# A layer of attention and two of a network in one kernel: first-layer weights summed on VectorE, products ahead of the first attention, another order of the steps

## The chip, the cores and the metric

The kernel runs on one core of one Trainium2 chip. The metric is the device time of one execution in microseconds (us). A core has TensorE (PE in the profile; its weight loads are PEld), VectorE (DVE), ScalarE (ACT), GpSimd (POOL) and SyncE (SP), each with its own queue of instructions, which it works through in order. DMA transfers are issued from SP, ACT and POOL.

## The reference

A gated linear attention is followed by two layers with a PReLU between them. All is float32. B = 4, H = 8, S = 768, D = 48; the network has 3072 tokens of width H*D = 384, and 2048 hidden units.

```python
f = 1.0 / (1.0 + np.exp(-f_logit))
for t in range(S):
    state = f[:, :, t, :, None] * state + np.einsum('bhd,bhe->bhde', k[:, :, t], v[:, :, t])
    y[:, :, t] = np.einsum('bhd,bhde->bhe', q[:, :, t], state)
x = y.transpose(0, 2, 1, 3).reshape(B * S, H * D)
h = x @ w_in
g = np.maximum(h, 0.0) + alpha * np.minimum(h, 0.0)
return g @ w_out
```

## The kernel before

The tokens are cut into chunks of C = 128, and two batch entries are worked on together. That gives 12 steps, `(bp, c)`: two pairs of batch entries in each of six chunks. A step has four stages, each a generator that yields between its parts:

- `prepare` (L260) loads q, k, f and v. It makes the products of the gates within groups of four tokens (`qd`, L289), two running products (`ps`, `ss`, L319 and L321), and scaled queries and keys (`us`, `k4`, `q3`, `kh`, `ks`; L323 to L408). In chunks after the first it transposes the keys on VectorE (`kt`, L424) and spreads them with 16 small DMAs from SP into `ksn` (L429). In first chunks `ksn` comes from TensorE transposes (`pk`, L473).
- `carry` (L434) has the products `off` (L446, and L456 in first chunks), copies them to the attention matrix `A` on ACT, and carries the state: products `pd` (L486), then `moved`, which updates `vs` (L496, L500; L502 on ACT in first chunks).
- `attend` (L508) has, for each of the two batch entries, the small products `raw` (L522) and `qu` (L537), which VectorE copies under masks into `ad` (L528, L543; L559 in first chunks). These PSUM tiles ("pair") have two buffers in rotation with `off`, `pk`, `pd` and `py`. ACT then copies `ad` to `A` (L565), `py` (L576) multiplies with `vs`, and `y` (L585) is brought to the network's layout `xT`: by products `xt` (L594) in step 0, by DMAs from SP and ACT (L604) later.
- `network` (L610) has eight parts f, each with products `ph` (L619) into a PSUM bank, one ReLU on ACT (L624) and two gates on VectorE (L626). Step 0 then uses plain products `po` (L639) with `w_out_sb`; later steps use seven products of half width (`pa` to `pe`, L658) with sums made on VectorE (L700, L671 to L685). The banks ("net") have four buffers in rotation.

The network of a step runs in the next step, beside the attention of that step and the first half of `prepare` of the one after. The order is written out by hand: `manual_schedule` keeps TensorE, VectorE and ACT to the order of the program, and a string of letters for each of the first four steps, `first`, and one for the rest, `usual`, says which generator goes on next. P is the rest of this step's `prepare`, O `carry`, S `attend`, n the network of the step before, Q the next step's `prepare`. A number repeats. `a` and `w` are the two halves of loading `w_in`, `b` and `v` those of `w_out`, and W makes the sums of `w_out` (L719) that the half-width products need.

The weights are loaded in eight pieces each. They come from DRAM as int16 words (SP, L196, four buffers `raw`), ACT makes two parts of the upper half of the bits (L201, L203), and VectorE makes `lead` (L209), the scaled rest (L222) and its `power` (L215). At last `lead` is added to the rest, in `both`: by VectorE (L227) for pieces under `at_once`, otherwise by an accumulating DMA from POOL (L229). `AT_ONCE` (L27) counts for `w_in` alone. Part f of the first network needs piece f of `w_in`; a quarter of its `po` needs two pieces of `w_out`.

## Time and profile before

| | us |
|---|---|
| median of 3 runs (lowest to highest) | 637.01 (636.58 to 639.63) |
| the profiled execution's own time | 638.33 |
| its span, first to last instruction | 636.5 |
| TensorE products busy | 589.7 (93%) |
| TensorE weight loads busy | 524.9 (82%) |
| VectorE busy | 505.8 (79%) |
| ACT busy | 249.6 (39%) |
| POOL busy | 67.6 (11%) |

Times in the profile count from the first instruction. A row of a timeline has the start, the time to the end of the group, the engine, the line, the operation, out<-in with their shapes, and how many instructions follow each other. In brackets stands the engine's idle time before them and what ended it; "issue" is time in which it waited for nothing that the profile shows. A row of the waits has the waiting line, what it waited for, the total in us, how often, and the longest. A row of the chain of waits has start, us, and what the end of the program depended on then. A float32 product of the program is recorded as two products; a transpose is recorded as one.

### The profile page before, as it was taken

The numbers are of one execution on the slowest core, as the hardware profiler recorded it, in microseconds if no ns is written. First come the engines' busy times: TensorE is split into PE (matmuls) and PEld (weight loads), VectorE is DVE, ScalarE is ACT, GpSimd is POOL, SyncE is SP. The second block draws the span as 40 slices with busy tenths as digits, with TensorE's granted clock in tenths as the row PEclk, the third lists the DMA queues.
The fourth block names the chain that finished last, engine by engine and source line by source line (L and its number), as shares of the span: only waits on it lengthen the run. The fifth ranks groups of instructions, "written<-read, shape, count | busy, mean of one in ns | idle before, by whom it ended". The sixth has DMA issues, their size and how long they took to land.

```text
span 636.5 us, 18857 instructions
## 1 busy us (share of the span) xinstructions
PE 589.7 (93%) x8108; PEld 524.9 (82%) x8108; DVE 505.8 (79%) x1028; ACT 249.6 (39%) x466; POOL 67.6 (11%) x114
## 2 busy tenths in 40 slices
PE   0449699989999999999999999999999999999997
PEld 0447576779889889889889889889889889889997
DVE  5879959999799788888888888888888888762251
ACT  5667673432254153253253253253253253223120
POOL 9133212001001001001001001001001000000000
PEclk9999989999999999999999999999999999999999
DMA  7978978233232323223233233223233211201000
GB/s 260 280 199 235 287 198 199 46 77 78 43 83 84 43 77 83 51 69 83 38 81 85 38 82 84 38 82 84 33 85 79 46 47 26 37 18 26 26 1 25
DMA packets 73122, 56.30 MB, mean 88 GB/s; under 512 B 47408, under 2 KB 64944, under 8 KB 73040
## 3 DMA queue, kind: packets, MB, share of 16 engines
q0 software_dynamic: 10112, 27.53, 16.4%
q1 hardware_dynamic: 57536, 25.37, 15.7%
q10 hardware_dynamic: 5392, 2.21, 1.7%
q8 instruction: 64, 1.05, 0.7%
q14 instruction: 18, 0.15, 0.1%
HBM read 36.21 MB, written 4.72 MB: 64 GB/s over the span
## 4 chain that ended last, share of the span: by engine, by line
PE 75%; DVE 14%; SPq 3%; issue 3%; ACT 2%; DMA 1%; DVEq 0%; ACTq 0%
PE ph L619 33%; PE pc L658 8%; PE pa L658 8%; PE pe L658 4%; PE pd L658 4%; PE pb L658 4%; SPq L429 3%; PE py L576 3%; PE raw L522 3%; PE qu L537 2%; PE pd L486 2%; DVE gate L626 1%; DVE ad L528 1%; DVE us L332 1%; DVE ad L543 1%
## 5 line engine op out<-in xcount | busy, mean ns | idle before, releaser
L619 PE MATMUL ph<-xT,w_in_sb 128*128 128x256 f32 x1152 | 260.9, 385 | 5.1 <-issue 4.9
L619 PEld LDWEIGHTS ph<-xT,w_in_sb 128*128 128x128 f32 x1152 | 218.2, 192 | 38.4 <-issue 7.3
L624 ACT ACTIVATE neg<-ph 128x512 f32<-128x512 f32 x96 | 57.1, 597 | 203.1 <-PE ph L619 144.0
L626 DVE SCALAR_TENSOR_TENSOR gate<-neg,om,ph 128x256 f32<-128x256 f32 x192 | 82.1, 476 | 48.4 <-ACT neg L624 48.2
L658 PE MATMUL pa<-w_out_sb,gate 128*128 128x192 f32 x352 | 62.1, 329 | 0.3 <-DVE gate L626 0.3
L658 PE MATMUL pc<-t,S 128*128 128x192 f32 x352 | 61.8, 329 | 0.1
L658 PEld LDWEIGHTS pa<-w_out_sb,gate 128*128 128x128 f32 x352 | 57.8, 190 | 2.2 <-DVE gate L626 1.3
L658 PEld LDWEIGHTS pc<-t,S 128*128 128x128 f32 x352 | 57.3, 190 | 1.1 <-DVE Csum L671 0.4
L528 DVE COPY_PREDICATED ad<-mraw,raw 128x256 f32<-128x256 int32 (+1 forms) x96 | 42.3, 440 | 8.3 <-PE raw L522 5.9
L543 DVE COPY_PREDICATED ad<-mquad,qu 128x224 f32<-128x224 int32 (+6 forms) x140 | 41.9, 299 | 6.2
L419 ACT COPY A<-q 48x512 f32<-48x512 f32 x44 | 27.2, 617 | 31.6 <-DVE q L370 31.2
L565 ACT COPY A<-ad 32x256 f32<-32x256 f32 x96 | 38.5, 401 | 1.4
L332 DVE TENSOR_TENSOR us<-us,fs 128x768 f32<-128x768 f32 (+5 forms) x60 | 37.0, 617 | 0.0
L289 DVE TENSOR_TENSOR qd<-qd,f 128x768 f32<-128x768 f32 (+2 forms) x36 | 27.2, 756 | 6.7 <-ACT qd L284 6.7
L576 PEld LDWEIGHTS py<-A,vs 128*64 128x64 f32 x768 | 25.5, 145 | 7.2 <-ACT A L565 4.3
L576 PE MATMUL py<-A,vs 128*64 128x64 f32 x768 | 27.5, 232 | 3.9 <-ACT A L565 3.9
L522 PEld LDWEIGHTS raw<-qd,k 48*32 48x32 f32 x1536 | 18.7, 109 | 14.9 <-issue 13.9
L700 DVE TENSOR_TENSOR S<-gate 128x512 f32<-128x512 f32 x44 | 30.3, 688 | 0.8
L676 ACT COPY o<-pa 128x192 f32<-128x192 f32 x11 | 3.5, 317 | 69.7 <-PE pa L658 65.4
L522 PE MATMUL raw<-qd,k 48*32 48x80 f32 x1536 | 23.9, 243 | 7.3 <-issue 5.6
L658 PE MATMUL pe<-w_out_sb,S 128*128 128x192 f32 x176 | 30.5, 327 | 0.0
L658 PE MATMUL pd<-w_out_sb,S 128*128 128x192 f32 x176 | 30.4, 326 | 0.0
(109 smaller groups left out, 749.8 us busy)
## 6 DMA issues: line engine op xcount, KB each, us to landing
w_out_raw<-in_w_out SPq DMA_DIRECT2D x8, 767.8 KB, 6.0
w_in_raw<-in_w_in SPq DMA_DIRECT2D x8, 767.2 KB, 5.8
f<-in_fT POOLq DMA_DIRECT2D x11, 512.0 KB, 4.4
q<-in_qT POOLq DMA_DIRECT2D x11, 512.0 KB, 4.0
k<-in_kT POOLq DMA_DIRECT2D x11, 512.0 KB, 5.1
out<-o SPq DMA_DIRECT2D x24, 192.0 KB, 2.1
vs<-in_v POOLq DMA_DIRECT2D x22, 192.0 KB, 5.2
w_out_sb<-w_out_lead POOLq DMA_DIRECT2D x8, 384.0 KB, 5.4
```

What stands on the lines that cost most here:

```text
L289: nc.vector.tensor_tensor(qdv[d], qdv[d - 1][:, :, :, 1:5 - d], f[:, :, 1:5 - d].rearrange("p (g i) r -> p g i r", i=NB), ALU.mult)
L332: nc.vector.tensor_tensor(us[:, :, UO[m]:UO[m] + 4 * n].rearrange("p g (i r) -> p g i r", r=4), us[:, :, skip:skip + 4 * n].rearrange("p g ...
L522: nc.tensor.matmul(raw[DB * j:DB * (j + 1), par, hp * C:hp * C + QW], lhsT=k[r_, g * DB:(g + 1) * DB], rhs=qd[r_, g], start=True, stop=True)
L528: nc.vector.copy_predicated(adu[:, :, :, d:4], mraw[:, d, :, d:4].bitcast(I32).unsqueeze(1).broadcast_to((128, H, NB, n)), rv[:, :, QO[d]: ...
L543: nc.vector.copy_predicated(ad[:, u, :, :, 4 * m:DB], mquad[:, lo:lo + n].bitcast(I32).unsqueeze(1).unsqueeze(1).broadcast_to((128, 2, HP, ...
L565: nc.scalar.copy(A[s_, u, :, s_], ad[s_, u].rearrange("p r h t -> p (r h) t"))
L576: nc.tensor.matmul(py[64 * par:64 * par + 64, u, o:o + CH], lhsT=vs[bp][:, cc, u, hd * D:hd * D + 64], rhs=A[:, u, par * HP + hp, CH * cc: ...
L619: nc.tensor.matmul(ph[:, j * T:(j + 1) * T], lhsT=w_in_sb[:, kt, m * 128:(m + 1) * 128], rhs=xT[:, kt], start=(kt == 0 and j == 0), stop=( ...
L624: nc.scalar.activation(neg, phv, AF.Relu, scale=-1.0)
L626: nc.vector.scalar_tensor_tensor(gate[:, m % NH, m // NH], neg[:, j], om[:, m:m + 1], phv[:, j], ALU.mult, ALU.add)
L658: nc.tensor.matmul(to[:, 0:DH], lhsT=of(f), rhs=by(f), start=(f == 0 and not more), stop=(f == NH - 1), skip_group_check=True)
L700: nc.vector.tensor_tensor(to, x_, y_, op)
```

## The change

Four things are changed. All eight pieces of `w_in` are summed on VectorE, none by an accumulating DMA; those of `w_out` stay as they are. Forty small products into a bank that no one reads stand ahead of everything else on TensorE; their operand `ones` is set by POOL. In chunks after the first, the transpose of the keys goes one stage of `prepare` up, right behind the last write to `ks`; the 16 DMAs behind it stay where they are. And the strings of the first four steps are another order of the same letters; `usual` is unchanged.

```diff
-AT_ONCE = 1
+AT_ONCE = 8
+IDLE = 40
...
         nc.vector.tensor_tensor(ks[:, :, 0], kh, f32[:, 1:G:2].broadcast_to((128, GC, DB)), ALU.mult)
         if c:
+            kt = x["kt"] = late["kt"].tile([128, W], F32, tag="kt", name=f"kt_{i}")
+            nc.vector.transpose(kt, ks.rearrange("p g s t -> p (g s t)"))
             earlier(7)
...
         if c:
-
-            kt = late["kt"].tile([128, W], F32, tag="kt", name=f"kt_{i}")
-            nc.vector.transpose(kt, ks.rearrange("p g s t -> p (g s t)"))
+            kt = x["kt"]
             ksn = x["ksn"] = work.tile([128, U, HP * 128], F32, tag="ksn", name=f"ksn_{i}", bufs=1)
...
+    idle = bank("idle")
+
     steps = [(bp, c) for c in range(NC) for bp in range(B // U)]
     first = (
-        "P2 a P w P a P a w O P w S a w S Q a O a w S2 Q w S Q S",
-        "P a w a P w2 b n2 v O n S b2 v n v n P S b S v n b n S v b v n Q b n b v O v Q n v W Q2 S2 W n Q n W Q W",
-        "O W n2 S n2 S Q S n4 O S Q n Q2 n S2 n Q n Q n",
-        "n2 S n S n Q n2 O Q O n2 S Q S n S Q n Q S Q n3",
+        "P2 a P w P a P a w O P w S a w S Q a S O a w S Q2 w S2",
+        "P a w a P w n b w n v O b v n b S v n2 P S b S v n b S v n b v n Q b n Q v b O v Q n v W Q S2 Q W n2 W Q W",
+        "O n2 S W n2 S Q S n4 O S n Q2 n Q2 S n S n Q n",
+        "S n3 S n Q n2 O Q O n2 S Q S n S Q n Q S Q n3",
     )
...
     with tc.manual_schedule(engines={mybir.EngineType.PE, mybir.EngineType.DVE, mybir.EngineType.Activation}):
+        for _ in range(IDLE):
+            nc.tensor.matmul(idle[0:32, 0:8], lhsT=ones[:, 0:32], rhs=ones[:, 0:8], start=True, stop=True)
         prep, car, att, net = begin(0)
```

## The prediction

> **What bounds the kernel now.** I read the waits of TensorE first, before and after 163 us.

> ```profile
> PE off L446 <- DVE q L370: 18.3, 1, 18.3
> PE raw L522 <- issue: 5.6, 2, 3.1
> PE ph L619 <- issue: 4.9, 1, 4.9
> ...
> PE qu L537 <- DVE ad L543: 2.0, 2, 1.5
> ```

> ```profile
> PE pd L486 <- DMA ksn<-kt: 0.9, 2, 0.6
> PE qu L537 <- DVE ad L543: 0.5, 1, 0.5
> ```

> After 163 us TensorE waits for under 2 us in 470. That part can't shrink, since its products stay. All that is to be won lies before.

> There the chain of waits, in order of time, has one long "issue" and then a change of engine:

> ```profile
> 72.96 4.88 issue
> 77.84 10.22 PE ph L619 x33
> 88.07 0.40 ACT A L565
> 88.48 1.01 ACT w_out_pos L201
> ...
> 90.88 0.98 DVE w_out_sb L222
> ```

> From 90.88 it stays on VectorE to 163. So in this stretch VectorE's queue sets the time, and what counts is how long VectorE idled earlier. Its timeline, read for idle time over 0.8 us (in brackets):

> ```profile
> 27.66 1.88 DVE L528 COPY_PREDICATED ad<-mraw,raw 128x256 f32<-128x256 int32 x4 [2.45 <-PE raw L522]
> ...
> 34.67 1.89 DVE L528 COPY_PREDICATED ad<-mraw,raw 128x256 f32<-128x256 int32 x4 [2.31 <-PE raw L522]
> ...
> 47.90 1.23 DVE L323 TENSOR_TENSOR us<-us,f 128x1024 f32<-128x1024 f32 x1 [1.92 <-ACT us L316]
> ```

> ```profile
> 84.05 0.87 DVE L626 SCALAR_TENSOR_TENSOR gate<-neg,om,ph 128x256 f32<-128x256 f32 x2 [5.14 <-ACT neg L624]
> 86.98 0.87 DVE L626 SCALAR_TENSOR_TENSOR gate<-neg,om,ph 128x256 f32<-128x256 f32 x2 [2.06 <-ACT neg L624]
> ```

> With 0.82 at 90.41 that is 6.7 early and 8.0 late, 14.7 us. Why was TensorE late? Its timeline:

> ```profile
> 23.23 0.75 PE L522 MATMUL raw<-qd,k 48*32 48x80 f32 x22
> 26.49 0.96 PE L522 MATMUL raw<-qd,k 48*32 48x80 f32 x38 [2.50 <-issue]
> ...
> 33.56 0.90 PE L522 MATMUL raw<-qd,k 48*32 48x80 f32 x38 [3.14 <-issue]
> ```

> Counted from the first, TensorE stops before recorded product 222 (64 + 128 + 8 + 22), then at 349 and 476, and at 1112: steps of 127, 127 and 5 x 127.2. A 16 KB packet of the instruction queue (64 packets, 1.05 MB on the page) runs 1.3 to 2.4 us ahead of each restart: at 24.1, 31.2, 36.3, 75.6. TensorE is waiting for its own program.

> [...] the trace has it dry after 222 products, so I take two blocks. [...] with the engines 0.8 to 1.1 busy, a block requested when the one before it arrived took 7.1 (26.49 to 33.56), 4.9 (to 38.46) and, for the one after 71.2, 6.6 us. [...] behind the 4.88 us the windows show clock 0.51 and 36 ph take 11.01 us, against 36 x 0.224 (24 in 5.38) = 8.1. The block behind 730 runs at 52.7, before product 603 (55.4) starts: dispatch runs ahead.

> **The change, part by part.**

> *Sums on VectorE.* Seven pieces more on L227, 0.95 us each; started back to back 0.86 apart (22.53 to 23.39): 7 x 0.86 = **+6.0 on VectorE**. Taken away: seven L229 of 1.3 us on POOL, whose queue holds the k and q loads (no one waits for these), and 7 x 384 KB of accumulating transfers, which landed after 8.1 us. What this does for the blocks' latency isn't shown: bounded by 7.2 (no relief) and 4.9 (least seen). I take 6.5.

> *Idle products.* 40 calls are 80 recorded products (raw has 32 calls a half, x64). They need only `ones`, so they run in the 18.3 us of idle; at the 58 ns of py early on (60 in 3.47) 4.6 us at most. Queued behind their wait is only off L446, itself waiting to 18.3: cost nothing; without that cover, the 4.6. But they move every block boundary 80 products earlier in the work. And they let dispatch [...] pass product 95 before 10 us, so the block from 222 on is fetched in the idle time. The boundaries that bite become 349 (in the first half's qu) and 476 (second half's qu). In step 1, raw and qu of the second half were exactly one block (985 to 1112 consumed in 1.5 us, hence the 4.88). Now 984 falls into qu of the first half, and block 984 to 1111 holds 24 ph, 5.4 us: the next has time to come.

> *Replay of step 0* (own estimates from the durations above). VectorE has its third piece at 25.13 + 0.86 = 26.0; raw is complete at 24.3; L528 runs 26.0 to 27.9. Block 349 is asked for at 20.5, there at 27.0; qu ends 28.1, L559 29.2. Next piece 2.6 (0.47 + 0.99 + 0.28 + 0.86): 31.8. L528 of the second half to 33.7. Block 476 at 27.0 + 6.5 = 33.5, qu 34.5, L559 ends 35.6, where it was 37.67. A copies of the first half (L565, 1.65 us on ACT) now come ahead of pd and its L502; pd isn't over before 35.7, so they fit. Then first products of prepare 3.6, piece 2.6, scans 1.3: 43.2. ACT has the us copies (L316, 2.1) done at 42.4: the 1.92 is gone. L323 to L355 2.9, piece 2.6, L496 and L500 2.1: 50.8 against 53.1. **2.3 gained**, with four of the seven new sums paid.

> *Step 1.* VectorE without idle: second half of prepare 3.15 + 2.25, pieces 2.6 + 2.6 + 1.85, eight pairs of gates 8 x 0.85 = 6.8, six first steps of w_out 0.87 + 5 x 1.75, two halves of attention 2.9 each: 50.8 + 34.7 = 85.5, where L292 started at 92.94. **7.4 gained.** The idle time gives the same: 14.7 - 6.0 - 1.2 (0.3 and 0.9 left above before the two L559) = 7.5. TensorE keeps up: f7 ends about 82, its gate is due at 84.6. The w_out pieces on SP and ACT do too: each transfer starts when `rest` of the fourth piece before it frees a buffer, lands some 6 us later and has 1.9 of ACT; the closest is piece 1, ready at 63.9 for 65.8. To 136.3 VectorE has the same work in another order, the W sums among it: still 7.4.

> *TensorE beside it.* po runs 82.2 to 106.5 (4 x 5.3, pd, py), then off and four ph: 112.8, where f1's gate is due at 113.4. Slack 0.6. The last accumulated w_out pieces (5.4 us to land) come 0.4 us ahead of their po.

> *Transpose sooner, other order.* kt (1.24 us) goes ahead of L332, L406, L370, L414: 2.2 us sooner in VectorE's queue, nothing added. Its 16 transfers stay in their stage on SP, behind xT's. It takes off the two waits on ksn, **0.9**. L680 to L682 come 1.2 later; the ph that wait for their banks come 1.3 or more behind, nothing. In step 2 the y copies go behind the third part of the network, so behind L676: 2.7 us later for y and the ten xT transfers on SP and ACT, which took 8.8 us from y to ph (154.1 to 162.97). The new string puts raw and qu (1.7) ahead of ph; **1.4 lost**. The 0.5 on L543 at 174 goes: raw is earlier.

> *Sum.* 7.4 - 1.4 + 0.5 + 0.9 = 7.4. The profiled span is 636.5 of its own run of 638.3 (1.8 around it), the median of the runs is 637.0. I take the difference off the median: **629.6 us**; the span would be 629.1.

> **Rivals.**
> - *Cold clock or late input.* TensorE now idles about 2.7 us at 55 (off waits for L404) and 1.9 at 64 (a block). For: 4.88 was enough before. [...] A half-speed window of 6.8 us costs 3.4, less slack 0.6 to 2.4: 1 to 2.8 lost, 631 to 632.5. 13%.
> - *Idle products don't pull the fetch.* If dispatch stops at the first wait, block 222 comes at 18.5 + 6.5 = 25.0, off and pk finish at 27, the second L559 ends at 40.0, 4.4 later than above: 634.0. Against: the block at 52.7. 10%.
> - *More than I see.* Blocks in 4.9 us (+1.2), xT not late (+1.4), PE waits of 126 to 163 gone with the new order: 626 to 627, at most 625. 10%.
> - *Slower.* The stall re-forms: blocks are asked for as late as before and dense raw and qu meet a boundary again. Then the 8.0 us around 84 stay. Four of the seven sums hide in the 6.7 of early idle; three lie on VectorE's chain: + 2.6, **639.6**. It decides from where less than 2.6 of the 8.0 comes back. Against: 24 ph of 5.4 us lie in the critical block by count. 7%.

> **How the numbers follow.** Forecast 60%, its own range 627 to 632: block latency 4.9 to 7.2 moves it by -1.2 to +1.2, xT by -1.4 to 0, slack of TensorE by +1. About 0.5% (3.2 us) is what a measurement of this kernel can tell from no change. Faster by more (under 633.8): forecast less 1 for its upper tail, the better case and the cold clock, 82%; within: that 1, the failed pull and 1 of the slower case, 12%; slower: 6%. Range: 626 to 634.5, which takes in half of the better case and half of the failed pull.

> **What would show it.** Right: no "issue" wait of 4.9 on ph L619 and no clock of 0.5 around 80; L528 of the first half at 26 and the second L559 done at 35.6; L227 x8; L292 of step 2 near 85.5; VectorE's idle between 20 and 92 down from 14.7 to about 2; ksn gone from TensorE's waits. Wrong: a new "issue" wait over 3 us in raw or qu; ph of step 3 waiting over 2 us for xT; VectorE waiting on raw at 26 to 35 as before.

## The result, and the profile after

| | median us | ratio to before |
|---|---|---|
| before, beside the changed kernel | 638.88 (636.58 to 639.75) | |
| changed kernel | 634.44 (633.43 to 635.43) | 0.9937 [0.9921, 0.9954] |
| changed kernel, measured again on another occasion | 633.61 (632.31 to 635.20) | 0.993 [0.9907, 0.9954] |

The changed kernel is 4.4 to 5.0 us faster. 7.4 was forecast. The profiled execution took 634.88 with a span of 633.1, where before had 638.33 and 636.5: 3.4 less. From L28 on, line numbers are one higher than before; in `prepare` up to three.

TensorE's waits in the changed kernel:

```profile
PE off L447 <- DVE q L371: 12.1, 1, 12.1
PE off L457 <- issue: 4.8, 1, 4.8
...
PE qu L538 <- issue: 3.0, 2, 1.7
...
PE qu L538 <- DVE vs L501: 1.1, 1, 1.1
```

The 4.9 of "issue" ahead of ph is gone, as forecast, and so are the 0.9 on ksn. But a new stall of 4.8 stands in `off` of step 0, and qu waits 1.1 for the state. TensorE's timeline shows where:

```profile
2.16 4.43 PE L747 MATMUL idle<-ones 128*32 128x8 f32 x80 [2.16 <-POOL ones L119]
18.68 1.08 PE L447 MATMUL off<-q,kh 48*32 48x32 f32 x64 [12.08 <-DVE q L371]
20.31 0.98 PE L457 MATMUL off<-us 48*32 48x16 f32 x79 [0.55 <-DVE us L407]
26.12 0.71 PE L457 MATMUL off<-us 48*32 48x16 f32 x49 [4.83 <-issue]
...
75.70 0.81 PE L538 MATMUL qu<-us,k 48*32 48x52 f32 x64
76.44 8.04 PE L620 MATMUL ph<-xT,w_in_sb 128*128 128x256 f32 x36
```

80 + 64 + 79 = 223: TensorE ran dry after its first 223 products, where the next block of instructions should long have been there. That block's packet is at 23.1 in the trace, 4.2 us after product 96 (223 less a block of 127) ran at 18.9. In step 1 ph follows qu at once and 36 of them take 8.04 us at a granted clock of 1.00, not 11.01 after a stall of 4.88 (0.50 from 77.1 to 83.9 us). VectorE's timeline says what became of its idle time:

```profile
30.15 1.86 DVE L529 COPY_PREDICATED ad<-mraw,raw 128x256 f32<-128x256 int32 x4 [3.75 <-PE raw L523]
33.00 1.01 DVE L560 COPY_PREDICATED ad<-mhalf,qu 128x224 f32<-128x224 int32 x3 [0.99 <-PE qu L538]
...
82.94 0.86 DVE L627 SCALAR_TENSOR_TENSOR gate<-neg,om,ph 128x256 f32<-128x256 f32 x2
...
86.99 0.56 DVE L210 TENSOR_TENSOR w_out_lead<-w_out_pos,w_out_neg 128x768 bf16<-128x768 bf16 x1 [0.68 <-ACT w_out_neg L204]
```

The gates no longer wait (5.14 and 2.06 before). The three brackets sum to 5.4 where before had 14.7. Of the 9.3 less, 6.0 are filled by the new sums; 3.3 stay, and the first gate product of step 2 (L293) starts at 89.51 where L292 started at 92.94: 3.4 sooner. 85.5 was forecast.

From here on I split each span at the start of that instruction: a **head** up to it and a **tail** from it to the start of the last product. Before has 92.94 and 539.87; the changed kernel 89.51 and 539.89 in its first profile, 86.91 and 539.92 in its second.

### The profile page after: what moved, and what is told of

It is laid out like the page before. It is cut to its first block, busy times and chain, and to the rows that moved or that the text cites. A ratio compares the mean times of both kernels' runs of the same rounds, so it can differ in the third digit from the quotient of the medians.

```text
span 633.1 us, 19007 instructions
## 1 busy us (share of the span) xinstructions
PE 593.9 (94%) x8188; PEld 529.2 (84%) x8188; DVE 512.0 (81%) x1035; ACT 249.8 (39%) x466; POOL 58.8 (9%) x107
## 4 chain that ended last, share of the span: by engine, by line
PE 73%; DVE 22%; issue 2%; ACT 1%; DMA 1%; DVEq 0%; ACTq 0%
PE ph L620 34%; PE pc L659 8%; PE pa L659 8%; PE pe L659 4%; PE pd L659 4%; PE pb L659 4%; PE qu L538 3%; PE py L577 3%; PE raw L523 3%; PE pd L487 2%; DVE gate L627 2%; DVE S L701 2%; DVE us L333 1%; DVE qd L290 1%; DVE ad L529 1%
## 5 line engine op out<-in xcount | busy, mean ns | idle before, releaser
L529 DVE COPY_PREDICATED ad<-mraw,raw 128x256 f32<-128x256 int32 (+1 forms) x96 | 42.3, 441 | 7.3 <-PE raw L523 4.8
L422 ACT COPY A<-q 48x512 f32<-48x512 f32 x44 | 27.2, 617 | 42.4 <-DVE q L371 38.4
L538 PE MATMUL qu<-us,k 48*32 48x112 f32 (+1 forms) x1536 | 27.1, 259 | 4.2 <-issue 3.0
L659 PE MATMUL pb<-t,gate 128*128 128x192 f32 x176 | 30.4, 326 | 0.0
L577 PE MATMUL py<-A,vs 128*64 128x64 f32 x768 | 28.1, 233 | 2.0 <-ACT vs L503 1.0
```

The lines of the kernel that those rows point to most:

```text
L529: nc.vector.copy_predicated(adu[:, :, :, d:4], mraw[:, d, :, d:4].bitcast(I32).unsqueeze(1).broadcast_to((128, H, NB, n)), rv[:, :, QO[d]: ...
L538: nc.tensor.matmul(qu[DB * j:DB * (j + 1), par, hp * QS + 4:hp * QS + QL], lhsT=k4[r_, g * DB:(g + 1) * DB], rhs=us[r_, g, 4:QL], start=Tr ...
L577: nc.tensor.matmul(py[64 * par:64 * par + 64, u, o:o + CH], lhsT=vs[bp][:, cc, u, hd * D:hd * D + 64], rhs=A[:, u, par * HP + hp, CH * cc: ...
L659: nc.tensor.matmul(to[:, 0:DH], lhsT=of(f), rhs=by(f), start=(f == 0 and not more), stop=(f == NH - 1), skip_group_check=True)
```

## The experiments

Theory at the start: the fetch in step 0 failed, its delay goes on to the end, and the order of the strings carries what was gained. Rivals: the sums on VectorE cost more than counted; the sooner transpose delays the products after it.

| kernel | median us | ratio to before | profiled run | head | tail |
|---|---|---|---|---|---|
| idle0: changed, no idle calls | 634.56 | 0.9957 [0.9934, 0.9979] | 634.01 | 88.71 | 539.78 |
| idle46: changed, 46 calls | 631.62 | 0.9895 [0.9860, 0.9930] | 632.46 | 86.45 | 540.53 |
| idle48: changed, 48 calls | 632.95 | 0.9918 [0.9887, 0.9950] | 633.79 | 88.19 | 540.13 |
| idle52: changed, 52 calls | 632.61 | 0.9920 [0.9892, 0.9948] | 632.80 | 87.08 | 540.23 |
| order_only: before with new strings | 635.11 | 0.9946 [0.9923, 0.9969] | 636.16 | 91.32 | 539.36 |
| before_idle40: before with 40 calls | 633.67 | 0.9924 [0.9896, 0.9952] | 633.79 | 88.06 | 540.24 |
| before_idle52: before with 52 calls | 633.07 | 0.9911 [0.9888, 0.9933] | 630.91 | 84.31 | 541.13 |
| before_sums8: before with the sums on VectorE | 634.13 | 0.9936 [0.9912, 0.9961] | 637.39 | 89.89 | 542.00 |
| sums1: changed, sums by DMA again | 633.58 | 0.9928 [0.9901, 0.9954] | 631.99 | 86.77 | 539.75 |
| sums1_idle52: the same, 52 calls | 631.65 | 0.9890 [0.9866, 0.9913] | 631.90 | 86.59 | 539.85 |
| old_order: changed, old strings | 637.72 | 0.9995 [0.9978, 1.0011] | 638.11 | 91.05 | 541.58 |
| order_two: changed, old strings in steps 2 and 3 | 635.08 | 0.9964 [0.9945, 0.9982] | 635.08 | 87.93 | 541.67 |
| kt_late: changed, transpose in its old place | 631.50 | 0.9892 [0.9868, 0.9916] | 630.36 | 87.91 | 536.99 |
| kt52: kt_late with 52 calls | 629.51 | 0.9870 [0.9843, 0.9898] | 631.92 | 86.33 | 540.13 |
| kt52s1: kt52 with sums by DMA | 629.06 | 0.9856 [0.9831, 0.9880] | 629.09 | 86.08 | 537.51 |
| kt_first: kt52s1, sooner transpose in steps 2 and 3 | 629.82 | 0.9870 [0.9844, 0.9896] | 629.09 | 84.96 | 538.66 |
| kt_usual: kt52s1, sooner transpose from step 4 on | 629.71 | 0.9870 [0.9846, 0.9894] | 629.43 | 85.88 | 538.08 |

Each ratio is taken with runs of before beside it. Head and tail are those of one execution, and its time is not always near the median: the profile of before_sums8 is its slowest run (3.3 above the median), that of kt52 too (2.4 above), that of before_idle52 its fastest (2.2 below). A difference of a few us between two heads is therefore weak evidence by itself.

Seven of the tails hold a stretch at clock 0.5: before_idle40 (92 to 95 us), old_order (120 to 123), before_idle52 (122 to 125), before_sums8 (125 to 132), kt52 (135 to 138), idle52 (136 to 140) and order_only (140 to 144). At most half of such a stretch is lost, an estimate: 1.7 of some 3.4 us, and 3.4 of some 6.8 in before_sums8. The other tails, before's and the changed kernel's too, have none.

**How far dispatch looks past a wait.**

```diff
-IDLE = 40
+IDLE = 52
```

idle0, idle46 and idle48 have 0, 46 and 48 in its place.

> The changed kernel with 52 idle calls (104 recorded products) in place of 40 (80). Theory F (fetch): the gain fell short because 80 idle products end 16 short of the block boundary at product 96, dispatch stops at off's wait on q, and so the block from product 223 on is asked for only at 18.9 us; its wait of 4.8 us then stands in L457. With 104 the boundary lies ahead of that wait: the block is fetched before 10 us, no issue wait in L457; the next boundary (350, the 46th product of the first raw) is asked for at about 20.8 and there at 26 to 27; first L529 at 26.5 to 27.3 (30.15 in the changed kernel), second L560 done at 35.5 to 36.5 (39.5), total 3 to 4 us less than the changed kernel: 630.5 to 631.5. Rival S (sums): the shortfall is the seven sums on VectorE; then this run is within 0.5 us of the changed kernel, 634.

> The changed kernel with no idle products. Theory F: block boundaries are again where they were before the change. In step 0 the wait moves back into raw (restart near 26.5), first L529 at 27.5, second L560 done at 36 to 37.5, two to three us sooner than in the changed kernel; but in step 1 the second half's raw and qu are one whole block again, so an issue wait of 2 to 5 us comes back ahead of ph[...]: total 634 to 637. Rival S: idle products play no part, total within 0.5 us of the changed kernel.

> The changed kernel with 46 idle calls: 92 recorded products, so the boundary at product 96 lies 4 products of off behind the products that wait for q. If nothing behind a wait is dispatched ahead, the block is asked for when off starts, some 18.5 us, its packet comes near 23, and off L456 stalls some 4 to 5 us as with 40 calls. If dispatch looks even a few products past a waiting one, the packet comes near 8.5 as with 52 calls and the stall is gone.

> The same with 48 idle calls: 96 recorded products, up to the boundary and not over it. If the block behind the next one is asked for when product 96 is handed out, and nothing is handed out behind the wait, the packet still comes near 23; if finishing the first 96 is enough, it comes near 8.5 and TensorE doesn't stall in off.

```profile
2.16 5.08 PE L747 MATMUL idle<-ones 128*32 128x8 f32 x92 [2.16 <-POOL ones L119]
...
20.25 1.43 PE L457 MATMUL off<-us 48*32 48x16 f32 x128 [0.55 <-DVE us L407]
...
28.13 0.42 PE L523 MATMUL raw<-qd,k 48*32 48x80 f32 x4 [3.39 <-issue]
```

All 128 products of L457 are one group. The stall isn't gone: it moves one block on, into raw, where it is shorter. The copy L560 of step 0's second half ends at 39.48 and 37.60 (40 calls, two profiles), 37.18 (46), 36.80 (48) and 35.70 (52); 35.6 was forecast. By the medians the early fetch is worth 0.7 to 2.8 us, less than the 3 to 4 that were expected of idle52; the intervals are too wide for more. No idle calls at all (idle0) give about the same time as 40, within the intervals: its ph of step 1 waits 2.4 on issue, but no `off` stalls, and its second L560 ends at 35.63. In the changed kernel the forty calls lose in step 0 about what they gain in step 1.

**One part alone on the kernel before.** order_only has the four new strings, before_idle40 and before_idle52 the idle calls with their bank, before_sums8 this:

```diff
-AT_ONCE = 1
+AT_ONCE = 8
```

> The kernel before with nothing but the four new strings: AT_ONCE = 1, no idle products, transpose late. Theory O: the strings carry the whole gain, and sums and idle products cancel out; then it is level with the changed kernel, 633.5 to 635.5. Theory F: without lighter DMA queues and without the shift of the blocks, the issue wait ahead of ph near 73 us is back at 4 to 5 us with the clock at half behind it (2.4 us and no half clock in the run with sums on VectorE and no idle products), which costs 2 to 4 us: 636.5 to 638.

> The kernel before with the 40 idle calls of the change and nothing else: 80 recorded products, so that no block is fetched ahead of off, but every boundary lies 80 products earlier in the work. If the place of the boundaries is what counts, the 4.9 us ahead of ph in step 1 go (the boundary then lies some 47 products into raw and the block before it holds 24 ph of 5.4 us), although step 0 is up to 2 later: a gain of 3 to 4, 634 to 635.5. If the early fetch is what counts, step 0 loses and step 1 does not gain: 637.5 to 639.

> The kernel before with 52 idle calls and nothing else. If the idle products' worth is the early fetch of the block at product 222, the second L560 ends near 35.6 here too, 2 us sooner than before, and the stall of 4.9 us ahead of ph in step 1 shrinks or moves, as the boundary then lies 22 products into raw: 634 to 636. If the gain needs the new order (VectorE's waits of the old order absorb it), step 0 is sooner and the end is not: 637 to 638.

> The kernel before with all pieces of the first layer's weights summed on VectorE, nothing else. Forecast's step: 6 more on VectorE, 3.4 of it in idle time, 2.6 on the path, unless the lighter DMA queues bring the blocks of instructions sooner. With no relief 639.5 to 640.5; with blocks some 2 us sooner at each of the stalls (as where the idle calls are left out of the changed kernel) 636 to 637.

Each of the four gains 2.8 to 5.5 us by itself, where the whole change gains 4.4 to 5.0. So the gains don't add. The sums and both numbers of idle calls work on the same stall, the one ahead of ph in step 1, and on VectorE's wait behind it. order_only is faster without removing it: it came out where Theory O had its time, but ph still waits 2.6 on issue, with the clock at half from 75.6 to 82.4, and its head is only 1.6 shorter. before_sums8 gained more than either of its cases. TensorE's timeline before, then with the sums alone:

```profile
71.46 0.92 PE L522 MATMUL raw<-qd,k 48*32 48x80 f32 x64
...
77.84 11.01 PE L619 MATMUL ph<-xT,w_in_sb 128*128 128x256 f32 x36 [4.88 <-issue]
```

```profile
72.62 0.92 PE L522 MATMUL raw<-qd,k 48*32 48x80 f32 x64
...
75.10 7.93 PE L619 MATMUL ph<-xT,w_in_sb 128*128 128x256 f32 x36 [0.98 <-issue]
```

The boundary lies where it lay before, between qu and ph, and the stall is 0.98, not 4.88. From the start of raw to ph it takes 2.5 us instead of 6.4: the block's packet comes 2.7 us sooner (72.9, before 75.6), and TensorE gets to the boundary 1.2 later. From 72 to 74 us the DMA engines are busy to 0.03, where before had 0.87. The head is 3.05 shorter although VectorE has 6 us more to do. 52 idle calls alone:

```profile
69.90 0.48 PE L523 MATMUL raw<-qd,k 48*32 48x80 f32 x24
70.67 0.70 PE L523 MATMUL raw<-qd,k 48*32 48x80 f32 x40 [0.29 <-issue]
...
71.89 5.23 PE L620 MATMUL ph<-xT,w_in_sb 128*128 128x256 f32 x23
```

Here the boundary has moved to 24 products into raw, behind 5.4 us of ph, and the stall is 0.29. The head is the shortest of all, 84.31, in a run 2.2 below its median. And 40 calls alone, which stall 4.6 in `off` like the changed kernel, have no stall in step 1 and a head 4.9 shorter: so moving the boundaries is worth that much without the early fetch. What 52 calls take off the head beyond it, 3.8, doesn't show in the medians, which are 0.6 apart. The rival expectation for 40 calls (637.5 to 639) fell.

**One part undone or changed.**

> The changed kernel with AT_ONCE = 1: seven of the eight sums go back to accumulating DMAs. Rival S: the seven sums, 0.86 us each, lie on VectorE's chain but for the one that ends at 26.4 in its idle time: 5 us less, 629.5. Theory F: VectorE's chain gets shorter by the same 5, but the accumulating transfers load the DMA engines again, so packets of instructions wait 3 to 4 us in place of 0.7 to 2 after 30 us, and the blocks of step 0 and 1 come later by some 2 us each: total 630 to 635.

> The changed kernel with AT_ONCE = 1 and 52 idle calls. If the two effects add up (spans: 52 calls 2.1 less than the changed kernel, AT_ONCE = 1 2.9 less): span 628 to 629, total 629.5 to 631. Rival: with the accumulating transfers back, blocks come later and TensorE or po waits for w_out pieces, so only one of the two counts: 631.5 to 633.

> The changed kernel with the four strings of before (idle products, sums on VectorE and sooner transpose kept). Both theories: TensorE's products in steps 0 and 1 keep their order, so the blocks fall as in the changed kernel; the A copies behind pd cost step 0 about 1.5 us of ACT's time where VectorE waits for L316 (1.9 before the change), the rest is within 1 us: 635 to 637. A rival, that the order is where the gain comes from: 638 or more, as much as before the change.

> The changed kernel with the strings of steps 0 and 1 new and those of steps 2 and 3 as before. All four strings old cost 3.4 us at pa of step 3, of which 1.5 were there at the first operation of step 2's prepare (L293), 2.3 at pe of step 2. If the steps hold their own share: level with the changed kernel up to L293 of step 2 (89.5), then 1.5 to 2 us later at pa of step 3, total 636 to 636.5. Rival: the later strings don't matter and all comes from steps 0 and 1: total within 0.5 us of the changed kernel.

> The changed kernel with the transpose of the keys back where it was. If the sooner transpose is worth the two waits on ksn: these waits (0.9 us in all) are back in TensorE's list and the total is 0.5 to 1 us more than the changed kernel, 635 to 635.5. Rival: it costs as much as it saves (from pa of step 3 to the last product the kernel before took 441.9 us, the changed one 442.5): 634.0 to 634.5, and this stretch takes 442.0 or less.

> The changed kernel, unchanged, beside the next three on one chip. If the 3 us between it and the version with the late transpose are a matter of the chip or of the run, this one ends near 632 and its second L560 ends near 38 instead of 39.5. If they belong to the transpose, it stays at 634 to 635 and still shows TensorE's wait of about 1 us in qu of step 3 on the copies of L501.

sums1: 633.58 against 634.44 and 633.61: no difference that the intervals carry, in either direction. In the changed kernel the sums cost about as much as they relieve. sums1_idle52 took 631.65, the case in which the two effects don't add up in full. old_order: the whole gain is gone (637.72, between its two expectations), so sums, idle calls and sooner transpose together need the new strings, though sums and idle calls gain alone. With the old strings VectorE waits 2.98 at 88 for a transfer of `w_out`, and py in step 0 waits 3.6 for the A copies. order_two: the head stays short (87.93), the tail is 541.67, so by these profiles the first two strings make the head and the other two some 1.8 of the tail. Its median, 0.6 to 1.5 above the changed kernel, lies between its two expectations and doesn't settle it.

The transpose:

```diff
-            kt = x["kt"] = late["kt"].tile([128, W], F32, tag="kt", name=f"kt_{i}")
-            nc.vector.transpose(kt, ks.rearrange("p g s t -> p (g s t)"))
...
-            kt = x["kt"]
+            kt = late["kt"].tile([128, W], F32, tag="kt", name=f"kt_{i}")
+            nc.vector.transpose(kt, ks.rearrange("p g s t -> p (g s t)"))
```

kt_late is 2.1 to 2.9 below the changed kernel, and its tail 2.9 shorter (536.99 against 539.89 and 539.92). after_again was to tell whether this was the chip: its head was 2.6 shorter than in the first profile, so heads do vary, but its tail repeated within 0.03 and the wait on L501 was there again.

**Without the sooner transpose, and where it costs.**

> Transpose back in its old place and 52 idle calls. If the two effects lie in different places (the fetch before 36 us, the transpose at pe of step 2 and later), they add up: 1.8 off the 52 calls alone and some 2 to 3 off the transpose, 629.5 to 630.5, with the second L560 done at 35.7 and the last product near 624. If both only move the same slack, it stays at 631.5, where the late transpose alone is.

> Transpose late, 52 idle calls and the sums of pieces 1 to 7 back on the accumulating DMAs, so that of the change only the order of the strings and (more) idle products are left. Theory (the sums on VectorE are a cost of about 1): 628.5 to 630, not above the run with the sums on VectorE. Rival (the accumulating transfers load the DMA engines and delay the blocks of instructions): up to 1.5 above it, 631 to 632.

> Order and 52 idle calls, sums on accumulating DMAs, and the transpose sooner in the second chunk's steps 2 and 3 alone. If the sooner transpose costs where a wait of TensorE on L501 is seen (160 us), this one loses 1 to 2 against the version with the late transpose, 630.5 to 631. If the cost is spread over the steady state, it stays within 0.5 of it, 629 to 629.5.

> The same with the transpose sooner in all steps from 4 on, and late in steps 2 and 3. If the cost is at steps 2 and 3, this one is equal to or up to 0.5 better than the all-late version (no waits on ksn): 628.5 to 629. If it is spread, 630 to 631.5, with short waits of TensorE on o or ksn in each step.

The two repairs add up: kt52 takes 629.51 and kt52s1, with new strings and 52 idle calls alone, 629.06. That is 4 to 5.4 below the changed kernel, and below each repair alone (632.61 and 631.50). Against idle52 and sums1_idle52 the late transpose is worth 3.1 and 2.6 by the medians. The profile of kt52 doesn't show it: its tail of 540.13, in its slowest run, has the half clock in it. TensorE's waits from 155 us on, first with the sooner transpose in steps 2 and 3 alone, then with none:

```profile
PE qu L543 <- DVE vs L506: 1.1, 1, 1.1
...
```

```profile
PE pd L486 <- DMA ksn<-kt: 0.7, 1, 0.7
...
```

The sooner transpose takes the waits on ksn away (0.7) and brings one of qu on the second state update (L506 there, L500 with the late transpose, L501 in the changed kernel). VectorE's timeline shows why, again first with the sooner transpose, then without:

```profile
150.20 1.25 DVE L404 STREAM_TRANSPOSE kt<-ks 128x1024 f32<-128x1024 f32 x1
...
154.96 1.12 DVE L506 TENSOR_TENSOR vs<-vs,pd 48x384 f32<-48x384 f32 x2
```

```profile
154.74 1.12 DVE L500 TENSOR_TENSOR vs<-vs,pd 48x384 f32<-48x384 f32 x2
...
156.82 1.24 DVE L424 STREAM_TRANSPOSE kt<-ks 128x1024 f32<-128x1024 f32 x1
```

Ahead of this qu VectorE is the queue that TensorE follows. 1.25 us of transpose ahead of the update is passed on to qu, where in its old place it stands behind the update and the sums. Product by product, kt_first is 1.15 us ahead of kt52s1 before this qu and 0.22 behind after it. The two end together (spans of 627.3), because the head of kt_first, which does the same work there, was 1.1 shorter; hence a tail of 538.66 against 537.51. kt_usual is 0.6 above, with a wait of 0.4 of pe on ACT's o. The changed kernel falls behind kt_late in the same places: 1.25 at this qu, 0.6 at a pe at 205. The last 1.0 of its 2.9 comes in small parts from 205 to 560, nearly all in qu, with no wait that the profile shows; it stays open. The medians of kt_first and kt_usual (0.8 and 0.7 above kt52s1) lie inside the intervals and between their expectations, so it is these traces that place the cost, not the times.

## Why the prediction was wrong

- **What bounds the kernel: right.** VectorE's queue to 163 us, TensorE starved by its own blocks, in steps of 127. The head was shorter than before's in every experiment.
- **Step 1's stall goes: right.** No issue ahead of ph, a clock of 1.00 behind it, no idle time at the gates.
- **The step that failed: that dispatch would "pass product 95 before 10 us".** 16 products lay between the end of the idle ones and product 96, and by the packets dispatch looked at least 4 but fewer than 16 past the wait. So `off` stalled 4.8, the second L560 ended 3.9 late in the first profile (2.0 in the second), and the head was 4.0 (1.4) longer than forecast. In the first profile that is the whole of the missing 4.0 us: forecast span 629.1, measured 633.1. It is the rival "Idle products don't pull the fetch", put at 634.0 and at 10%. My ground against it was the block that ran at 52.7 before product 603 started. But ph starts at 53.84, and 603 comes 1.5 us or 7 products later: the trace showed a look past ph's wait of at most 7 products, where the forecast needed one of 16. That count was there to be made; that the look goes as far as 16 was my assumption. It is not the whole miss: where the fetch works, idle46, idle48 and idle52 still take 631.6 to 633.0, where 629.6 was forecast.
- **Step 0's replay: right where the fetch works.** With 52 calls the two L560 end at 29.29 and 35.70; 29.2 and 35.6 were forecast.
- **Sums, "7 x 0.86 = +6.0 on VectorE": right; the relief for the blocks, "I take 6.5": too little.** It was bounded by 4.9 to 7.2 us for a block. The DMA engines weren't 0.8 to 1.1 busy all through these waits, as I wrote: from 30 to 32 and 32 to 34 us before has 0.58 and 0.25. With the sums alone the block of step 1 took 2.5 us from raw to ph, where before took 6.4, and the kernel gained by them. In the changed kernel, where that stall is gone anyway, they gain nothing that the intervals carry.
- **Transpose sooner, 0.9 gained: wrong in sign.** The ksn waits went as forecast, but it costs 2 to 3 by the medians. I followed L680 to L682 and found their delay covered; L501, 1.25 us behind the transpose too, wasn't followed to qu.
- **Order, 1.4 lost and 0.5 gained: too low.** With the transpose late, the new strings' tails are 537.0 (kt_late) and 537.5 (kt52s1) against 539.9; order_only and kt52 have 539.4 and 540.1 with a stretch at half clock. Some 2.4 to 2.9 us gained made up for the transpose: that the tail came out as forecast (no change) is luck, two errors of opposite sign.
- **The rival "Cold clock": in part.** In the first profile TensorE waited 2.81 for L407 ahead of 61.8, and its clock was at half from 62.8 to 66.2; in the second it waited 2.05 and kept its clock. VectorE has no idle time from 34 to 86 us in the first, so no loss by it is shown.

So by the medians the kernel lost 0.7 to 2.8 us to the missed fetch and 2.1 to 2.9 to the transpose, and with both repaired it takes 629.5. The runs show the step that failed in the first; of the second, 1.25 and 0.6 are located and about 1 us is not.

## What to carry to other kernels

Here the stalls for instructions sat at fixed counts of instructions (127 recorded products or a multiple of it apart), so anything that shifts the count, lightens the DMA queues or reorders the work could remove or shorten them, and several such changes didn't add up. Before counting on dispatch to run ahead, count in the trace how many instructions behind a waiting one the fetch was triggered. An operation moved up a queue can delay everything that it passes: follow each of these to who waits for it, and try each part of a change alone, since here one part hid a loss of 2 to 3 us. And see where the profiled execution lies among the runs before comparing stretches of two profiles.

## What the runs showed of the hardware

If a block is asked for when the product one block (127) ahead of its start is handed out, the packets say that TensorE was handed at least 4 and fewer than 16 recorded products behind a waiting one (a packet at 9.4 us with 4 between, at 23.1 with 16). Identical code varied by 2.6 us in its head between two profiles, 1.9 of it by the second L560, where blocks of instructions came later. Before, the clock halved at 77.1 us, 4.1 into the wait of 4.88, and stayed at 0.50 to 83.9. The forecast counted no loss from waits of 2.7 and 1.9, which no trace had shown to be safe: the clock halved during or just after waits of 1.83 at 133 us in kt52, 2.04 at 134 in idle52, 2.62 at 74 in order_only and 2.81 at 59 in the changed kernel. But the changed kernel waited 1.8 for the same gate as kt52 and kept a clock of 1.00 (130 to 142 us), so the length of one wait doesn't decide it.
